# Order of the first loads and first products, and the queue of six stores, in an attention and MLP kernel

## The chip, the core and the metric

The kernel runs on one core of one Trainium2 chip. A core has TensorE (PE, matrix products into the PSUM memory), VectorE (DVE), ScalarE (ACT), GpSimd (POOL) and SyncE (SP). Each takes its instructions in program order and waits for others through semaphores. DMAs are issued from an engine's queue, here SP's and ScalarE's, and are carried out by 16 DMA engines. The metric is device microseconds of one execution; less is better.

## What is computed

One transformer block over 2048 rows of 512 numbers, in float32:

```python
x = A_x                                                  # 1 x 2048 x 512
h  = x + attention(layernorm(x), wqkv) @ wo              # 32 heads of 16, softmax over all 2048 keys
h2 = h + silu(layernorm(h) @ w1) @ w2                    # w1: 512 x 1792, w2: 1792 x 512
```

## The kernel before

Every float32 operand of a product is split into a high part and a low part (the rest), and a product is made as three: high by high, low by high, high by low. `low` (line 123) is the subtraction that makes a low part. The helpers `mm`, `tr`, `act`, `dve`, `pool`, `dma` (SP's queue) and `dma_beside` (ScalarE's queue), lines 97 to 121, pin each instruction to its place in program order on its engine, so the order of the calls in the text is the order of the work. The profile gives the helper's line: L98 is a matrix product, L101 a transposition on PE, L105 GpSimd, L112 ScalarE, L115 VectorE, L118 and L121 DMA issues from ScalarE and SP.

The rows are worked in four blocks of 512, each of four tiles of 128 rows.

**The start (lines 636 to 730).** The first block is made apart, with float32r operands, so that PE has work early. SP issues 20 loads of 256 KB: four tiles of x (`load_x`), four chunks of the values' weights (`raw_v`, 128 of the 512 input features each), eight chunks of the weights of keys and queries, and four tiles of the second block of x. The order of the first eight is x tile 0, x tile 1, value weight 0, x tile 2, value weight 1, x tile 3, value weights 2 and 3. In the trace x of this block lies in a buffer called `ks`, the raw weights in one called `va`. Then:

- `idle(20)` and `idle(4)` transpose the identity matrix on PE; their results are not used.
- `statistics` (line 211) takes mean and variance of a tile on VectorE (`bn_stats`, `bn_aggr`) and their reciprocal deviation on GpSimd (two small instructions into `rs`).
- `first_rows(t)` normalizes tile t on VectorE, turns it on PE (four transpositions) and casts it out of PSUM on ScalarE into `xth0` (`xt_h` in the trace).
- The four chunks of the values' weights are cast to float32r (`wv0_h`): chunks 0 and 3 on GpSimd, 1 and 2 on ScalarE. `low_v(c)` makes their low parts `wv0_l` on VectorE.
- `first_products(t, chunks)` adds the products of the high parts of tile t and of the chunks named into the PSUM bank of tile t. They are made by chunk: chunks 0 and 1 for tiles 0 and 1, chunk 2 for both, chunks 0 to 2 for tile 2, chunk 3 for tiles 0 to 2, all four for tile 3.
- The statistics of tiles 2 and 3 follow the normalization of the tile ahead of each. The low parts of weight chunks 0 and 1 stand between these steps, those of chunks 2 and 3 and of the four tiles of x at the end.

After that PE makes the products with the low parts (line 716 on), ScalarE evacuates the values and squares the raw weights, whose sums give the scales, and the second block's tiles are turned.

**The attention and MLP loop (line 1337 on).** PE makes scores, ScalarE exponentials, PE the products with the values; the maxima of the scores of later heads are found beside it by PE and VectorE (`maximum`, line 280; `mx` in the trace). When the heads of a block of rows are done, the block's MLP is run by `mlp(b)` (line 1114), for the first three blocks; the last has `finish_last`. `mlp` makes 14 chunks of first products, then second products in two passes over the 14 chunks: pass 0 for row tiles 0 and 1, pass 1 for tiles 2 and 3 (`pair_seconds`, line 1079, and `last_seconds`, line 1091). Bursts of maxima are put between them (`insert`, line 1145). The weights of the MLP lie split in DRAM (`w1d`, `w2d`) and are loaded over SP's queue, through a ring of eight buffers (`raw_tile`, tile `w`): a load waits until PE has left the buffer eight loads back. Pass 1 loads the second weights again.

`add_seconds` (line 1072) adds a finished tile to the rows on VectorE and issues the store of 256 KB to `out`; in pass 0 it is called at chunk 13 for each of two tiles, in `last_seconds` for the other two. All these stores go over SP's queue; only the second half of the very last tile (`m` = 1) goes over ScalarE's. `at["beside"]` is a flag that `mlp` sets at the head of each pair of chunks: true in all of pass 0 and in the first pairs of pass 1 (chunk below 4), false after that and everywhere else. `place_far` (line 333), which sends maxima through DRAM, already picks its queue by it.

Of the kernel before, what the change touches and what calls it, by code (L numbers as in the profile page):

```python
# [20 lines left out]
P = 128  # L21
# [5 lines left out]
DC = D // P  # L27
# [11 lines left out]
LN = 2.0 ** 10  # L39
# [51 lines left out]
def attention_mlp_kernel(ctx: ExitStack, tc: tile.TileContext, x, wqkv, wo, w1, w2, out):  # L91
    nc = tc.nc
    x = x.flatten_outer_dims()
    out = out.flatten_outer_dims()


    def mm(*a, **k):
        tc.keep_in_program_order(nc.tensor.matmul(*a, **k))  # L98

    def tr(*a):  # L100
        tc.keep_in_program_order(nc.tensor.transpose(*a))  # L101


    def pool(op, *a, **k):
        tc.keep_in_program_order(getattr(nc.gpsimd, op)(*a, **k))  # L105


    def pin(ins):
        tc.keep_in_program_order(ins)

    def act(fn, *a, **k):
        pin(getattr(nc.scalar, fn)(*a, **k))  # L112

    def dve(fn, *a, **k):
        pin(getattr(nc.vector, fn)(*a, **k))  # L115
# [4 lines left out]
    def dma(*a):  # L120
        pin(nc.sync.dma_start(*a))  # L121

    def low(dst, src, high, engine="dve"):

        if high.dtype == F32R:
            high = high.bitcast(F32)
        (pool if engine == "pool" else dve)("tensor_tensor", dst, src, high, ALU.subtract)
# [40 lines left out]
    def bank(kind="st", dtype=F32):  # L168
        ps = space[:, next_bank(kind), :]
        return ps if dtype == F32 else ps.bitcast(dtype)[:, :512]  # L170
# [40 lines left out]
    def statistics(rows, scale=1.0):  # L211

        st = small.tile([P, 6], F32, name="st", bufs=5)
        mv = small.tile([P, 2], F32, name="mv", bufs=5)
        rs = small.tile([P, 1], F32, name="rs", bufs=5)
        dve("bn_stats", st, rows)
        dve("bn_aggr", mv, st)
        pool("tensor_scalar", rs, mv[:, 1:2], EPS, scale ** -2, op0=ALU.add, op1=ALU.mult)
        pool("tensor_tensor", rs, rs, expo, ALU.pow)
        return mv, rs  # L220

    def normalize(dst, rows, mv, rs, engine="dve"):
        (pool if engine == "pool" else dve)("tensor_scalar", dst, rows, mv[:, 0:1], rs, op0=ALU.subtract, op1=ALU.mult)
# [142 lines left out]
    at = {"item": 0, "done": 0, "half": 0, "step": 0, "due": 0, "attention": False, "group": None, "ready": 0, "next": 0, "blocks": True, "beside": False}  # L366
# [102 lines left out]
    with ExitStack() as pa:  # L469
# [13 lines left out]
        wv0_h, wv0_l, xth0, xtl0 = (wvp.tile([P, DC, 512], F32R, name=name) for name in ("wv0_h", "wv0_l", "xt0_h", "xt0_l"))  # L483

        xts = [ks[2 + b % 2].rearrange("p a n -> p (a n)").bitcast(F32).rearrange("p (t d) -> p t d", d=D)
               for b in range(NB)]
# [3 lines left out]
        flat = va.rearrange("p c h d -> p (c h d)")  # L490
        raw_v, *raw_qk = (flat[:, -n * DC * D:][:, :DC * D].rearrange("p (c n) -> p c n", c=DC) for n in (3, 2, 1))

        def load_x(b, parts=1, tiles=range(4)):
            n = 4 // parts
            for t in tiles[::n]:
                r0 = b * 512 + t * P
                dma(xts[b][:, t:t + n, :], x[r0:r0 + n * P, :].rearrange("(t p) d -> p t d", p=P))

# [132 lines left out]
        def turn_x(b, t):  # L631

            turn(xts[b][:, t, :], xth[b][:, :, t * P:(t + 1) * P], xtl[b][:, :, t * P:(t + 1) * P],
                 "sm" if b == 1 else "st")

        load_x(0, 4, range(1))
        for dc in range(DC):
            load_x(0, 4, range(4)[dc + 1:dc + 2])
            dma(raw_v[:, dc, :], wqkv[dc * P:(dc + 1) * P, 2 * D:])
        for key in (1, 0):  # L640
            for dc in range(DC):
                dma(raw_qk[key][:, dc, :], wqkv[dc * P:(dc + 1) * P, key * D:(key + 1) * D])
        load_x(1, parts=4)


        def columns(t):
            return slice(t * P, (t + 1) * P)

        def idle(n):
            ps = bank()  # L650
            for c in range(n):
                tr(ps[:, columns(c % 4)], ident, ident)

        def turn_high(b, t):
            ps = bank("sm").rearrange("p (c n) -> p c n", n=P)
            high = xth[b] if b else xth0
            for c in range(4):
                tr(ps[:, c, :], xts[b][:, t, c * P:(c + 1) * P], ident)
            act("copy", high[:, :, columns(t)], ps)
            return ps  # L660

        idle(20)
        found = [statistics(xts[0][:, t, :], LN) for t in range(2)]
        turned, ps_vs = [], []

        def first_rows(t):
            normalize(xts[0][:, t, :], xts[0][:, t, :], *found[t])
            turned.append(turn_high(0, t))

        def first_products(t, *chunks):  # L670
            if t == len(ps_vs):
                ps_vs.append(bank("st" if t < 3 else "sm"))
            for c in chunks:
                mm(ps_vs[t], xth0[:, c, columns(t)], wv0_h[:, c, :], start=c == 0, stop=False)

        def low_v(c):
            low(wv0_l[:, c, :], raw_v[:, c, :], wv0_h[:, c, :])

        first_rows(0)
        pool("tensor_copy", wv0_h[:, 0, :], raw_v[:, 0, :])  # L680
        idle(4)
        first_rows(1)
        act("copy", wv0_h[:, 1, :], raw_v[:, 1, :])
        found.append(statistics(xts[0][:, 2, :], LN))
        low_v(0)
        for c in range(2):
            for t in range(2):
                first_products(t, c)
        act("copy", wv0_h[:, 2, :], raw_v[:, 2, :])
        first_rows(2)  # L690
        found.append(statistics(xts[0][:, 3, :], LN))
        low_v(1)
        pool("tensor_copy", wv0_h[:, 3, :], raw_v[:, 3, :])
        for t in range(2):
            first_products(t, 2)
        first_products(2, 0, 1, 2)
        first_rows(3)
        for t in range(3):
            first_products(t, 3)
        first_products(3, *range(DC))  # L700
        for c in range(2, 4):
            low_v(c)
        for t in range(4):
            low(xtl0[:, :, columns(t)], turned[t], xth0[:, :, columns(t)])

# [4 lines left out]
        found = {}  # L710
# [24 lines left out]
        for b in range(NB):  # L735
# [6 lines left out]
            found = {}  # L742
# [81 lines left out]
        for g in range(1, NG // 2):  # L824
            for m, (b, key) in enumerate([(b, 1) for b in range(NB)] + [(b, 0) for b in range(NB)]):
# [3 lines left out]
                n = 8 * g + m - 12  # L829
# [3 lines left out]
                beside = {BESIDE_A1[m]: 6} if g == 1 and m < len(BESIDE_A1) else BESIDE_A  # L833
                if n >= 18:
                    beside = BESIDE_T[n - 18]
# [206 lines left out]
    def rows_of(b, t):  # L1042
        return ot[b % 2][:, t].rearrange("p c n -> p (c n)")
# [28 lines left out]
    def add_seconds(b, t, ps, m=0, parts=1):  # L1072

        n, h = 4 * b + t, rows_of(b, t)
        cols = slice(m * D // parts, (m + 1) * D // parts)
        dve("scalar_tensor_tensor", h[:, cols], ps, out_f, h[:, cols], op0=ALU.mult, op1=ALU.add)
        (dma_beside if m else dma)(out[n * P:(n + 1) * P, cols], h[:, cols])

    def pair_seconds(b, acc, tiles, f, gates):

        w2 = [ws.pop(("w2", k)) for k in (f, f + 1)]
        for t in tiles:
            rows = slice(t * P, (t + 1) * P)
            for k, ((gh, gl), (w2h, w2l)) in enumerate(zip(gates[f:f + 2], w2)):
                for x, w in ((gh, w2h), (gl, w2h), (gh, w2l)):
                    mm(acc[t], x[:, rows], w, start=f + k == 0 and w is w2h and x is gh, stop=f + k == FC - 1 and w is w2l)
                    yield
            if f + 2 == FC:
                add_seconds(b, t, acc[t])
# [85 lines left out]
    found = {}  # L1175
# [138 lines left out]
    def maxima(g):  # L1314

        i, c = divmod(g, KC)
        goals = [(64 * (n + 1), KC * n) for n in range(i + 1, LAST)]
        goals += [(END - 32 * (1 - a), KC * LAST + HALF * a) for a in range(2) if KC * LAST + HALF * a > g]
        ready = min(ITEMS, i + RING - (0 if c == KC - 1 else 1)) * 64
        rate = max([(n - sum(x for x, m in zip(BESIDE, marks) if g <= m <= start) - at["done"])  # L1320
                    / max(1, start - AHEAD - g) for n, start in goals] or [0])
        if ready < END:
            rate = min(rate, (ready - at["done"]) / (KC - 1 - c or KC))
        at["due"] += max(0, rate)
        if g < LAG or g in marks or g - 1 in marks:

            return 0
        at["ready"] = ready
        most = 2 if at["step"] in late or c == JOINT and i and i - 1 not in FIRSTS else 3
        n = max(0, min(most, int(at["due"]), ready - at["done"]))  # L1330
        at["due"] -= n
        return n
# [4 lines left out]
    for g in range(groups):  # L1337
        tick()
        i, c = divmod(g, KC)
# [13 lines left out]
        if i in FIRSTS:  # L1353
            b, n = i // 8 - 1, c - OUTPUT
# [23 lines left out]
        n = maxima(g)  # L1378
# [4 lines left out]
        beside = range(n)  # L1383
        if n == 3 and more < 0:
            beside = range(1, 4)
        if n == 2 and more > 0:
            beside = 0, 2
# [52 lines left out]
```

## Time and profile before

| | |
|---|---|
| median of 3 runs | 1601.46 us (1600.91 to 1601.49) |
| the profiled execution | 1600.8 us |
| its span, first to last instruction | 1599.0 us |
| granted clock of TensorE | 1.00 |
| DMA, mean over the span | 86 GB/s |

In the rows of a timeline the first column is the start in microseconds from the span's start, the second the duration; then engine, line, operation and tiles, how many instructions are merged, and in brackets the idle time ahead of it and what ended it. A row of the waits reads: who waited for whom, us in total, times, longest. A row of a stretch gives its length and then the busy time of PE, PE's weight loads, VectorE, ScalarE and GpSimd, each with its number of instructions, the granted clock, the share of the DMA engines and GB/s.

### The profile page before, as it was taken

Reading aid. Unit: us, or ns where it says so; the run is one execution under the profiler, and the core shown is the slowest. Engines: PE = TensorE matmul, PEld = TensorE weight load, DVE = VectorE, ACT = ScalarE, POOL = GpSimd, SP = SyncE. Lnnn points to the kernel's source line nnn. Section 1 sums busy time; section 2 is a strip of 40 time slices with the busy share of each in tenths; the row PEclk is TensorE's granted clock in tenths of the full one; section 3 lists DMA queues with packets and bytes.
Section 4 is the critical chain, followed back from the end, with each engine's and each line's share of the span. In section 5 each row is a group of like instructions: output and inputs, shape, how many; then the busy total and the mean of one; then the engine's idle time right before and its main releaser. Section 6 shows DMA issues by size and latency. Waiting matters only on the chain.

```text
span 1599.0 us, 28492 instructions
## 1 busy us (share of the span) xinstructions
PE 1585.4 (99%) x10524; PEld 478.1 (30%) x10524; DVE 1389.5 (87%) x2053; ACT 1206.8 (75%) x2385; POOL 472.8 (30%) x755
## 2 busy tenths in 40 slices
PE   9999999999999999999999999999999999999999
PEld 6433322222234322222233322222234322222254
DVE  7999999999989889999989889999987789998432
ACT  5545799999964179999973179999974189999732
POOL 5643544544426101211135201211126101211200
PEclk9999999999999999999999999999999999999999
DMA  6667533442423521121123421112123511100222
GB/s 212 169 174 224 139 86 90 112 129 77 114 72 100 150 55 35 38 56 38 50 75 100 143 62 33 39 44 50 49 76 106 159 39 37 34 12 22 74 86 73
DMA packets 111427, 137.15 MB, mean 86 GB/s; under 512 B 29136, under 2 KB 66064, under 8 KB 111288
## 3 DMA queue, kind: packets, MB, share of 16 engines
q1 hardware_dynamic: 105844, 126.74, 28.8%
q10 hardware_dynamic: 5444, 8.59, 1.9%
q8 instruction: 82, 1.34, 0.4%
q14 instruction: 57, 0.47, 0.1%
HBM read 104.68 MB, written 24.85 MB: 81 GB/s over the span
## 4 chain that ended last, share of the span: by engine, by line
PE 83%; ACT 9%; DVE 5%; issue 1%; DMA 1%; POOL 1%; SPq 0%; POOLq 0%; ACTq 0%
PE ps L98 82%; ACT pt L112 9%; DVE mx L294 2%; DVE mx L296 1%; PE ps L101 1%; DVE pvs L115 0%; POOL rs L105 0%; DVE st L115 0%; DVE htl L115 0%; DVE hx L115 0%; DMA w<-w2d 0%; DMA md<-mt 0%; DVE ks L115 0%; POOL wv_l L105 0%; DMA ks<-in_A_x_dram 0%
## 5 line engine op out<-in xcount | busy, mean ns | idle before, releaser
L112 ACT ACTIVATE pt<-ps 128x512 f32<-128x512 f32 x2048 | 1009.0, 616 | 148.7 <-PE ps L98 146.7
L296 DVE TENSOR_REDUCE mx<-ps 128x1 f32<-128x512 f32 x1470 | 924.7, 683 | 51.6 <-PE ps L98 23.3
L98 PE MATMUL ps<-pt,va 128*17 128x512 f32 x4096 | 537.6, 598 | 0.9
L98 PE MATMUL ps<-qs,ks 64*128 64x512 f16 x2048 | 531.6, 380 | 2.4 <-DVE htl L115 0.7
L98 PE MATMUL ps<-ks,qs 48*128 48x512 f16 x2048 | 493.9, 381 | 1.5 <-DVE mx L294 1.1
L294 DVE TENSOR_REDUCE mx<-ps 128x2 f32<-128x1024 f32 x289 | 334.9, 1218 | 43.1 <-PE ps L98 41.8
L98 PEld LDWEIGHTS <-ks 64*128 64x128 f16 x2048 | 149.8, 95 | 545.5 <-issue 429.1
L105 POOL TENSOR_TENSOR ri<-rc,minus 128x16 f32<-128x16 f32 x31 | 90.7, 2925 | 235.3 <-DMA rc<-dn 168.7
L98 PE MATMUL ps<-w,gh 128*128 128x512 f16 (+1 forms) x678 | 154.6, 378 | 1.0 <-DMA w<-w2d 1.0
L98 PEld LDWEIGHTS <-qs 48*128 48x128 f16 x2048 | 126.6, 95 | 76.1 <-issue 59.7
L98 PEld LDWEIGHTS ps<-pt,va 128*17 128x17 f32 x4096 | 69.2, 95 | 223.6 <-issue 205.0
L98 PE MATMUL ps<-hth,w 128*128 128x512 f16 (+1 forms) x472 | 133.0, 370 | 0.0
L112 ACT ACTIVATE g<-ps,factors 128x512 f32<-128x512 f32 x56 | 38.4, 686 | 123.8 <-PE ps L98 96.7
L105 POOL TENSOR_TENSOR mx<-mx 128x32 f32<-128x32 f32 x52 | 12.4, 239 | 395.9 <-DVE mx L296 389.3
L98 PEld LDWEIGHTS <-w 128*128 128x128 f16 x708 | 66.2, 98 | 80.1 <-issue 12.5
L98 PEld LDWEIGHTS <-gh 128*128 128x128 f16 x678 | 63.0, 98 | 83.1 <-issue 13.7
L98 PE MATMUL ps<-htl,w 128*128 128x512 f16 (+1 forms) x236 | 84.1, 369 | 0.0
L115 DVE SCALAR_TENSOR_TENSOR gh<-g,factors,gh 128x512 f16<-128x512 f32 x14 | 10.5, 752 | 52.1 <-ACT gh L112 52.1
L112 ACT ACTIVATE ks<-ps 128x512 f32<-128x512 f32 x30 | 17.9, 598 | 49.2 <-PE ps L98 43.4
L105 POOL TENSOR_TENSOR sl<-ks,sh 128x512 f16<-128x512 f32 x30 | 34.6, 1156 | 51.6 <-ACT sh L112 32.5
L105 POOL TENSOR_TENSOR gh<-g,gh 128x512 f16<-128x512 f32 x42 | 48.5, 1155 | 3.5
L105 POOL TENSOR_TENSOR ot<-ot,den 128x512 f32<-128x512 f32 (+1 forms) x16 | 20.4, 1275 | 89.2 <-DMA den<-dr 72.8
(154 smaller groups left out, 974.3 us busy)
## 6 DMA issues: line engine op xcount, KB each, us to landing
w<-w2d SPq DMA_DIRECT2D x98, 256.0 KB
ks<-kd SPq DMA_DIRECT2D x120, 192.0 KB
w<-w1d SPq DMA_DIRECT2D x56, 256.0 KB
ks<-in_B_w_dram ACTq DMA_DIRECT2D x28, 256.0 KB
w<-in_B_w_dram SPq DMA_DIRECT2D x28, 256.0 KB
qs<-qd SPq DMA_DIRECT2D x128, 48.0 KB
kd<-sh SPq DMA_DIRECT2D x16, 256.0 KB
qd<-sh SPq DMA_DIRECT2D x16, 256.0 KB
```

Of the source, the lines that this page charges most:

```text
L98: tc.keep_in_program_order(nc.tensor.matmul(*a, **k))
L101: tc.keep_in_program_order(nc.tensor.transpose(*a))
L105: tc.keep_in_program_order(getattr(nc.gpsimd, op)(*a, **k))
L112: pin(getattr(nc.scalar, fn)(*a, **k))
L115: pin(getattr(nc.vector, fn)(*a, **k))
L294: pin(nc.vector.tensor_reduce(of, space[:, n:n + 2, :], axis=AX.X, op=ALU.max))
L296: pin(nc.vector.tensor_reduce(of[:, j:j + 1], space[:, n, :], axis=AX.X, op=ALU.max))
```

## The change

It has two parts. In the start, x's four tiles are all loaded ahead of the four chunks of the values' weights. The statistics of tile 2 now stand ahead of the normalization of tile 1, those of tile 3 ahead of the normalization of tile 2. Weight chunk 0 is cast on ScalarE, chunk 1 on VectorE, chunks 2 and 3 on GpSimd. The first products follow the tiles as they come, and all four low parts of the weights are made at the end on VectorE. In the MLP, `add_seconds` also uses ScalarE's queue while the flag is true: that holds for the two stores of pass 0, in each of three blocks.

```diff
-        def load_x(b, parts=1, tiles=range(4)):
+        def load_x(b, parts=1):
             n = 4 // parts
-            for t in tiles[::n]:
+            for t in range(0, 4, n):
...
-        load_x(0, 4, range(1))
+        load_x(0, parts=4)
         for dc in range(DC):
-            load_x(0, 4, range(4)[dc + 1:dc + 2])
             dma(raw_v[:, dc, :], wqkv[dc * P:(dc + 1) * P, 2 * D:])
...
-        def low_v(c):
-            low(wv0_l[:, c, :], raw_v[:, c, :], wv0_h[:, c, :])
-
         first_rows(0)
-        pool("tensor_copy", wv0_h[:, 0, :], raw_v[:, 0, :])
         idle(4)
+        found.append(statistics(xts[0][:, 2, :], LN))
+        act("copy", wv0_h[:, 0, :], raw_v[:, 0, :])
         first_rows(1)
-        act("copy", wv0_h[:, 1, :], raw_v[:, 1, :])
-        found.append(statistics(xts[0][:, 2, :], LN))
-        low_v(0)
-        for c in range(2):
-            for t in range(2):
-                first_products(t, c)
-        act("copy", wv0_h[:, 2, :], raw_v[:, 2, :])
+        found.append(statistics(xts[0][:, 3, :], LN))
+        first_products(0, 0)
         first_rows(2)
-        found.append(statistics(xts[0][:, 3, :], LN))
-        low_v(1)
-        pool("tensor_copy", wv0_h[:, 3, :], raw_v[:, 3, :])
+        dve("tensor_copy", wv0_h[:, 1, :], raw_v[:, 1, :])
+        for c in range(2, 4):
+            pool("tensor_copy", wv0_h[:, c, :], raw_v[:, c, :])
+        first_products(1, 0)
         for t in range(2):
-            first_products(t, 2)
-        first_products(2, 0, 1, 2)
+            first_products(t, 1)
+        first_products(2, 0, 1)
         first_rows(3)
         for t in range(3):
+            first_products(t, 2)
+        first_products(3, 0, 1, 2)
+        for t in range(4):
             first_products(t, 3)
-        first_products(3, *range(DC))
-        for c in range(2, 4):
-            low_v(c)
+        for c in range(DC):
+            low(wv0_l[:, c, :], raw_v[:, c, :], wv0_h[:, c, :])
         for t in range(4):
             low(xtl0[:, :, columns(t)], turned[t], xth0[:, :, columns(t)])
...
-        (dma_beside if m else dma)(out[n * P:(n + 1) * P, cols], h[:, cols])
+        (dma_beside if m or at["beside"] else dma)(out[n * P:(n + 1) * P, cols], h[:, cols])
```

## Prediction, made before the changed kernel was seen

> **What bounds the kernel now.** I read the head of the page first, then the waits of PE over the whole run, then PE's busy time in stretches.
>
> ```profile
> span 1599.0 us, 28492 instructions
> ...
> PE 1585.4 (99%) x10524; PEld 478.1 (30%) x10524; DVE 1389.5 (87%) x2053; ACT 1206.8 (75%) x2385; POOL 472.8 (30%) x755
> ```
> ```profile
> PE ps L98 <- DVE mx L294: 1.1, 4, 0.3
> PE ps L98 <- DMA w<-w2d: 1.0, 1, 1.0
> ```
> ```profile
> 5.00:10.00 5.00, 4.50 (x22) 3.06 (x22) 3.63 (x8) 2.21 (x4) 2.77 (x6) 1.00 1.03 379
> 10.00:15.00 5.00, 4.16 (x20) 2.64 (x20) 4.24 (x8) 2.10 (x3) 1.67 (x3) 1.00 1.05 391
> ```
>
> The reader is to see that TensorE has work nearly always: 1599.0 - 1585.4 = 13.6 us without it. So an edit can win only where PE waits, or where PE is kept from its next piece of work by an order of instructions. Two such places touch this change: the first 15 us (0.50 and 0.84 us without work in the two stretches shown, at a granted clock of 1.00), and one wait of 1.0 us for a second-product weight, the only one in the run. The profiled execution took 1600.8 us, 1.8 us around its span; the median shown, 1601.46, lies 0.66 above it. Differences are worked out on the trace and taken from the median.
>
> **Part 1: the start.** First the DMAs. SP issues all 20 loads of the start in one line; the change moves the third and fourth tiles of x from places 4 and 6 to places 3 and 4, and the four value weights from 3, 5, 7, 8 to 5, 6, 7, 8. Nothing else in SP's queue moves.
>
> ```profile
> 0.72 0.86 SPq L121 DMA_DIRECT2D ks<-in_A_x_dram  x2
> ...
> 3.52 6.26 SPq L121 DMA_DIRECT2D va<-in_A_wqkv_dram  x10
> ```
> ```profile
> GB/s 0 33 281 315 184 371 383 369 379 391 399 395 385 389 385 387 381 391 371 102 16 0 0 0 0 0 0 0 112 282 53 313 385 360 301 37 0 102 106 111
> ```
>
> The second fence has 1 us per number. Each transfer is 0.262 MB, so the running sum reaches transfers 3, 4, 5, 6, 7, 8 at about 4.9, 5.6, 6.3, 7.0, 7.7 and 8.4 us. The first is full by the sum at 2.8 us; VectorE first reads it at 3.44 us, 0.6 later, so I add 0.6 for landing (estimate): x's third tile at 5.5, its fourth at 6.2, the weights at 6.9, 7.6, 8.3, 9.0. The stream then runs on at the same rate to 19 us whatever the order of its first eight.
>
> Now the engines, each in order:
>
> ```profile
> 5.31 0.55 DVE L115 TENSOR_SCALAR ks<-ks,mv,rs 128x512 f32<-128x512 f32 x1 [0.17 <-POOL rs L105]
> 6.31 0.81 DVE L115 TENSOR_SCALAR ks<-ks,mv,rs 128x512 f32<-128x512 f32 x1 [0.45 <-POOL rs L105]
> 7.04 0.68 DVE L115 BATCH_NORM_STATS2 st<-ks 128x6 f32<-128x512 f32 x1
> 7.75 0.18 DVE L115 BATCH_NORM_AGGREGATE mv<-st 128x2 f32<-128x6 f32 x1
> ...
> 9.24 0.55 DVE L115 TENSOR_SCALAR ks<-ks,mv,rs 128x512 f32<-128x512 f32 x1 [0.72 <-POOL rs L105]
> ...
> 11.92 0.81 DVE L115 TENSOR_SCALAR ks<-ks,mv,rs 128x512 f32<-128x512 f32 x1 [0.72 <-POOL rs L105]
> 12.65 1.28 DVE L115 TENSOR_TENSOR wv_l<-va,wv_h 128x512 fp32r<-128x512 f32 x2
> 13.86 2.47 DVE L115 TENSOR_TENSOR xt_l<-ps,xt_h 128x512 fp32r<-128x512 f32 x4
> ```
> ```profile
> 5.63 0.64 POOL L105 TENSOR_TENSOR rs<-rs,expos 128x1 f32<-128x1 f32 x1
> 6.23 0.61 POOL L105 CAST wv_h<-va 128x512 fp32r<-128x512 f32 x1
> 8.03 0.55 POOL L105 TENSOR_SCALAR rs<-mv 128x1 f32<-128x1 f32 x1 [1.19 <-DVE mv L115]
> 8.66 0.55 POOL L105 TENSOR_TENSOR rs<-rs,expos 128x1 f32<-128x1 f32 x1
> ```
> ```profile
> 6.91 0.58 ACT L112 CAST xt_h<-ps 128x512 fp32r<-128x512 f32 x1 [4.91 <-PE ps L101]
> ...
> 8.35 1.14 ACT L112 CAST wv_h<-va 128x512 fp32r<-128x512 f32 x2
> ...
> 13.48 0.59 ACT L112 CAST xt_h<-ps 128x512 fp32r<-128x512 f32 x1 [2.35 <-PE ps L101]
> ...
> 21.18 1.07 ACT L112 ACTIVATE va<-ps 128x512 f32<-128x512 f32 x2
> ```
> ```profile
> 12.79 0.66 PE L101 MATMUL ps<-ident,ks 128*128 128x128 f32 x4 [0.64 <-DVE ks L115]
> 13.20 2.12 PE L98 MATMUL ps<-wv_h,xt_h 128*128 128x512 f32 x7
> 15.16 1.07 PE L98 MATMUL ps<-wv_l,xt_h 128*128 128x512 f32 x4
> 16.07 1.07 PE L98 MATMUL ps<-wv_h,xt_l 128*128 128x512 f32 x4
> ...
> 22.42 1.03 PE L101 MATMUL ps<-ident,ks 128*128 128x128 f32 x8
> ```
>
> The chain before: for each tile VectorE takes statistics, GpSimd makes the reciprocal deviation, VectorE normalizes, PE turns. The statistics of a tile stand right ahead of its own normalization, so GpSimd's two steps (8.03 to 9.21) lie open on VectorE, with a low part put between. The change puts the statistics of tile 3 ahead of the normalization of tile 2, and so on, and sends all four low parts behind. By the rows:
>
> - Tile 3's statistics follow the first normalization (5.86): 0.68 + 0.18, to 6.70. Its x, at 5.5, is there.
> - Second normalization 6.72 to 7.27: 0.55, as GpSimd casts nothing beside it now (0.81 when it did). Before it ended at 7.12: 0.15 lost.
> - Fourth tile's statistics to 8.1. GpSimd's steps for tile 3 (0.55 + 0.55) end at 8.0, so the third normalization runs 8.1 to 8.7 (before 9.24 to 9.79).
> - The new VectorE copy of a weight, 128x512: no row of its own. Below it can't be nothing; the nearest rows are 0.55 (the normalization, the same shape from SBUF) and 0.64 (1.28 for two subtractions). I take 0.55, to 9.25, with 0.3 to 0.8 as ends. The copy on ScalarE costs 1.14 / 2 = 0.57, at 7.5 behind the first turned tile, off the chain.
> - GpSimd's steps for tile 4 run 8.15 to 9.3; fourth normalization 9.35 to 10.15 (0.81, since the two GpSimd casts start beside it), before 11.92 to 12.73.
> - PE: turned tile 2 from 7.3, first product 8.1, turned tile 3 from 8.75, its cast done 1.28 after (13.48 + 0.59 - 12.79), at 10.0; two products; turned tile 4 from 10.5 (before 12.79).
> - Its cast is done at 11.8; seven products are left behind it, where four were. Four products take 16.07 - 15.16 = 0.91, so seven take 1.6. The first product with a low weight starts at 13.5, before 15.16: **1.65 us earlier**.
>
> What could be late next: the four low weights on VectorE, 10.15 + 4 x 0.64 = 12.7, before 13.5. The low rows follow (0.62 each) from 12.7, first needed at 13.5 + 0.91. ScalarE's run of casts and squares, which ended with the pair at 21.18 close ahead of PE's 22.42, starts 13.48 - 11.2 = 2.3 earlier. The second block's x keeps landing until 17, 0.6 behind the sum, and its second normalized tile is needed by PE at 20.8. From there all work hangs on PE's products, so the gain stays.
>
> A row to weigh a rule on: the normalization takes 0.81 instead of 0.55 where it runs beside GpSimd's cast (6.31 against 6.23 to 6.84). The Trainium skill, SBUF — State Buffer, Who interferes with whom, says that VectorE copies and tensor-scalars in their two-port mode and GpSimd block each other for a whole instruction. The trace agrees: 6.84 + 0.28 = 7.12, the end of that row. This speaks against moving a copy to VectorE and two casts beside it; at worst, by that rule, the fourth normalization loses to both casts, 9.3 + 1.22 + 0.28 = 10.8, and the gain is 1.3.
>
> So part 1 is worth -1.65, with ends 0 (the copy, the locks and the landings each at their worst) and -2.3 (all that the fourth turned tile gains).
>
> **Part 2: the stores.** Six stores of 256 KB, two in each of three blocks, go from SP's queue to ScalarE's.
>
> ```profile
> 1264.58 0.61 PE L98 MATMUL ps<-ks,qs 48*128 48x512 f16 x4
> ...
> 1273.06 0.38 PE L98 MATMUL ps<-w,gh 128*128 128x512 f16 x1 [1.00 <-DMA w<-w2d]
> ```
> ```profile
> 1264.77 1.73 ACTq L118 DMA_DIRECT2D md<-mt  x4
> ...
> 1265.39 3.26 SPq L121 DMA_DIRECT2D out_dram<-ot  x2
> ...
> 1267.54 0.74 DVE L115 SCALAR_TENSOR_TENSOR ot<-ps,factors,ot 128x512 f32<-128x512 f32 x1
> 1268.00 0.54 ACTq L118 DMA_DIRECT2D qs<-md  x2
> 1268.74 7.63 SPq L121 DMA_DIRECT2D w<-w2d  x9
> ...
> 1273.80 3.49 DVE L294 TENSOR_REDUCE mx<-ps 128x2 f32<-128x1024 f32 x3 [1.56 <-PE ps L98]
> ...
> 1284.35 2.06 ACT L112 ACTIVATE pt<-ps 128x512 f32<-128x512 f32 x4 [39.09 <-PE ps L98]
> ```
>
> This is the third block. SP sits on the second store until VectorE has added the rows (1267.54 + 0.74), and only then issues the load that PE waits for: 1268.74 to 1273.02, 4.3 us. That load is the weight of chunk 5 of the second pass, and takes the buffer of chunk 11 of the first, which PE leaves some 12 products ahead of the four at 1264.58, at about 1261.9. With the stores gone from SP it is issued there; even at 4.3 us it lands by 1266.2, 6 us early. The next two loads need chunks 12 and 13, free by 1264.6, and are wanted after 1273.8. **1.0 us** goes. Its successor would be VectorE, which waits 1.56 us for PE there and about 0.4 at the other bursts, so no new wait of PE is due. In the first two blocks PE never waits for this weight (the row with 1 wait in the run): nothing is won there.
>
> On ScalarE two DMA issues of some 0.4 us stand behind the two of the maxima (done 1268.54), so the stores go out up to 3 us later; nothing reads them. Behind them is the exponential of 1284.35, after 39.09 us of waiting for PE: that cover of 15 us hides the wait for VectorE's addition; if it were gone, each block would pay up to the 3 us for which SP sat there. Part 2 is -1.0, with ends 0 and -1.0.
>
> **Sum:** -1.65 - 1.0 = -2.65; 1600.8 - 2.65 = 1598.15 by the profiled execution, 1601.46 - 2.65 = 1598.8 by the median.
>
> **Rivals.**
> - *The stores' move saves nothing.* The bytes still share the engines, and a wait of the same size follows. Against it: the stream there is no wall, SP is held by VectorE and not by bytes. The time: 1601.46 - 1.65 = 1599.8. The Trainium skill, DMA: Bandwidth & Descriptors, Issuing engines are not separate DMA queues, says that another issuing engine saves only issue time; what SP loses here is a wait in front of the issue, which that rule doesn't count. Chance 0.1.
> - *The start gives nothing:* the port locks and the longer tail of seven products eat the shorter chain. For it: three more products stand behind the last cast. Against it: 2.3 us of chain against 0.7 of products. The time: 1601.46 - 1.0 = 1600.5. Chance 0.1.
> - *The start gives all:* turned tile 4 and the tail both at their best, -2.3 - 1.0 or a little more, 1598.1. Chance 0.12.
> - *Slower: the value weights land late.* VectorE's copy of the second weight stands ahead of the fourth normalization and of every low part, so a weight that lands after 8.7 holds all of VectorE. To lose the 2.65 and 3.2 us more, the last weight must land some 6 us behind its need at about 12.6: 18.5. That is 2.1 MB in 16 us, 130 GB/s. The lowest microsecond of the stream has 184, among 315 and 371; a lasting fall is not to be seen. The time: 1601.46 + 3.4 = 1604.9. Chance 0.04.
>
> **How the numbers follow.** The forecast, both parts near the sums above, has 0.64, the rivals 0.1, 0.1, 0.12 and 0.04. Predicted 1598.8. The range goes from 1597.8 (both best ends, -3.3, and 0.35 for the spread of the runs) to 1600.8 (only one part, and the spread); it leaves out the slower rival and the tails. About 0.2%, 3.2 us, is what a measurement of this kernel can tell from no change: 1598.26 and below is faster. The fourth case and the lower quarter of the forecast, some 0.1 + 0.1, lie there: 0.2. Slower 0.04; the rest, 0.76, is within it.
>
> **What would show it.** In the profile after: the low-weight products start near 13.5 and the eight turns of 22.42 near 20.8; VectorE's normalizations at about 6.7, 8.1 and 9.4; PE's wait for the second-product weight is gone, and the load ahead of it stands near 1260 on SP; six stores on ScalarE's queue, its exponentials no later against PE. Wrong would be: a VectorE row before 9 us whose idle time is ended by a value weight's DMA, a PE wait for VectorE's maxima in place of the one removed, or a start gained by 21 us that is no longer there at 100.

## The result, and the profile after

The changed kernel takes 1598.55 us (median of 18 runs, 1598.02 to 1599.25) where the kernel before takes 1601.53 us beside it (18 runs, 1600.76 to 1602.51): a ratio of 0.9982, with a 95% interval of 0.9974 to 0.9989. That is 3.0 us less; 1598.8 was forecast, and the time lies within 0.2% of before. The profiled execution took 1598.55 us, with a span of 1596.7 us, 2.3 less than the span of before.

The head of the page after and the waits of PE over the whole run (who waited for whom, us in total, times, longest):

```profile
span 1596.7 us, 28487 instructions
...
PE 1585.3 (99%) x10524; PEld 477.6 (30%) x10524; DVE 1389.7 (87%) x2054; ACT 1207.2 (76%) x2384; POOL 472.6 (30%) x755
```
```profile
PE ps L101 <- POOL ident masks.py:199: 1.5, 1, 1.5
PE ps L98 <- DVE mx L294: 1.0, 4, 0.3
PE ps L101 <- DVE hx L115: 0.8, 4, 0.3
PE ps L98 <- ACT wv_h L112: 0.7, 1, 0.7
PE ps L98 <- DVE htl L115: 0.7, 3, 0.2
```

PE does the same work in the same busy time; 11.4 us of its span are empty now, 13.6 before. The wait for a second-product weight is gone from the list, and a new one of 0.7 us for the cast of a value weight stands in it.

The start, first as busy time by stretch, then the rows of VectorE, ScalarE and PE that answer to those of before:

```profile
5.00:10.00 5.00, 4.25 (x25) 3.38 (x24) 4.19 (x11) 2.00 (x4) 3.76 (x8) 1.00 0.99 361
10.00:15.00 5.00, 5.00 (x23) 3.61 (x22) 5.00 (x9) 3.75 (x6) 1.25 (x3) 1.00 1.05 388
```
```profile
5.51 0.55 DVE L115 TENSOR_SCALAR ks<-ks,mv,rs 128x512 f32<-128x512 f32 x1 [0.17 <-POOL rs L105]
5.97 0.69 DVE L115 BATCH_NORM_STATS2 st<-ks 128x6 f32<-128x512 f32 x1
...
6.79 0.52 DVE L115 TENSOR_SCALAR ks<-ks,mv,rs 128x512 f32<-128x512 f32 x1
...
8.23 0.51 DVE L115 TENSOR_SCALAR ks<-ks,mv,rs 128x512 f32<-128x512 f32 x1
8.72 0.43 DVE L115 CAST wv_h<-va 128x512 fp32r<-128x512 f32 x1
9.59 0.81 DVE L115 TENSOR_SCALAR ks<-ks,mv,rs 128x512 f32<-128x512 f32 x1 [0.45 <-POOL rs L105]
10.33 2.90 DVE L115 TENSOR_TENSOR wv_l<-va,wv_h 128x512 fp32r<-128x512 f32 x4
```
```profile
8.05 0.62 ACT L112 CAST wv_h<-va 128x512 fp32r<-128x512 f32 x1 [0.30 <-DMA va<-in_A_wqkv_dram]
```
```profile
8.72 0.50 PE L98 MATMUL ps<-wv_h,xt_h 128*128 128x512 f32 x1 [0.70 <-ACT wv_h L112]
...
10.91 0.60 PE L101 MATMUL ps<-ident,ks 128*128 128x128 f32 x4
11.26 2.81 PE L98 MATMUL ps<-wv_h,xt_h 128*128 128x512 f32 x10
13.91 1.07 PE L98 MATMUL ps<-wv_l,xt_h 128*128 128x512 f32 x4
...
21.17 1.03 PE L101 MATMUL ps<-ident,ks 128*128 128x128 f32 x8
```

The idle time ended by GpSimd ahead of VectorE's third normalization (0.72 before) is gone; the fourth starts at 9.59 where it started at 11.92. From 10 to 15 us PE has no empty time left by the profile's count (it was busy for 4.16 of the 5 us before). The products with the low weights start at 13.91 instead of 15.16, and the eight turns at 21.17 instead of 22.42: 1.25 us in this execution. The gain stays: the reload of ScalarE's table at the first MLP, first in before, then in after,

```profile
475.69 1.28 ACT L112 ACT_TABLE_LOAD   x1
```
```profile
474.45 1.28 ACT L112 ACT_TABLE_LOAD   x1
```

is 1.24 us earlier still. The third block's second products after, all engines:

```profile
1256.87 17.21 SPq L121 DMA_DIRECT2D w<-w2d  x12
...
1267.02 0.54 ACTq L118 DMA_DIRECT2D qs<-md  x2
...
1267.62 3.49 DVE L294 TENSOR_REDUCE mx<-ps 128x2 f32<-128x1024 f32 x3 [0.46 <-PE ps L98]
1267.65 0.85 ACTq L118 DMA_DIRECT2D out_dram<-ot  x2
...
1271.51 3.49 DVE L294 TENSOR_REDUCE mx<-ps 128x2 f32<-128x1024 f32 x3 [0.40 <-PE ps L98]
...
1282.07 2.07 ACT L112 ACTIVATE pt<-ps 128x512 f32<-128x512 f32 x4 [37.91 <-PE ps L98]
```

SP issues twelve weight loads on end, with no store between; the stores go out from ScalarE behind the two transfers of the maxima, and its next exponential still waits 37.91 us for PE. From one burst of maxima to the next VectorE counts 1271.51 - 1267.62 = 3.89 us, where before it was 1273.80 - 1268.75 = 5.05: 1.16 us less. That is the idle microsecond and 0.16 beside it.

### The profile page after: what moved, and what is told of

It reads as the page before. It is cut to its first block, busy times and chain, and to the rows that moved or that the text cites. A ratio compares the mean times of both kernels' runs of the same rounds, so it can differ in the third digit from the quotient of the medians.

```text
span 1596.7 us, 28487 instructions
## 1 busy us (share of the span) xinstructions
PE 1585.3 (99%) x10524; PEld 477.6 (30%) x10524; DVE 1389.7 (87%) x2054; ACT 1207.2 (76%) x2384; POOL 472.6 (30%) x755
## 4 chain that ended last, share of the span: by engine, by line
PE 71%; ACT 22%; DVE 4%; DMA 1%; issue 1%; POOL 1%; SPq 0%; POOLq 0%; ACTq 0%
PE ps L98 70%; ACT pt L112 22%; DVE mx L294 2%; DVE mx L296 1%; PE ps L101 1%; DMA va<-in_A_wqkv_dram 0%; DMA ks<-in_A_x_dram 0%; DVE st L115 0%; DVE htl L115 0%; DVE hx L115 0%; SPq L121 0%; POOL rs L105 0%; POOL wv_l L105 0%; DVE xtl L115 0%; DVE ot L115 0%
## 5 line engine op out<-in xcount | busy, mean ns | idle before, releaser
L98 PEld LDWEIGHTS <-gh 128*128 128x128 f16 x678 | 63.1, 98 | 83.0 <-issue 13.7
```

## Experiments

Each kernel was timed against before on the same chip, 11 runs each. The intervals are about 0.0009 wide to each side, 1.4 us, so a difference of one microsecond is read from the traces, and the times are only asked not to contradict them. "First low product" is the start of the first product with a low weight; "wait" is PE's wait for the second-product weight of the third block.

| kernel | median, before beside it (us) | ratio, interval | span | first low product | wait |
|---|---|---|---|---|---|
| start_only | 1599.12, 1601.13 | 0.9988, 0.9978 to 0.9997 | 1597.8 | 13.84 | 0.7 |
| stores_only | 1599.73, 1601.13 | 0.9992, 0.9983 to 1.0001 | 1598.5 | 15.09 | none |
| order_only | 1600.18, 1601.13 | 0.9994, 0.9985 to 1.0003 | 1599.2 | 14.03 | 1.6 |
| loads_only | 1601.46, 1601.13 | 1.0004, 0.9995 to 1.0013 | 1599.0 | 15.28 | 0.9 |
| statistics_only | 1600.37, 1601.10 | 0.9996, 0.9987 to 1.0005 | 1599.0 | 14.72 | 1.5 |
| statistics_and_turn | 1600.21, 1601.78 | 0.9993, 0.9984 to 1.0002 | 1598.7 | 14.02 | 1.2 |
| wait_no_bytes | 1600.04, 1600.74 | 0.9995, 0.9986 to 1.0004 | 1598.2 | 15.53 | 0.2 |
| twice_the_bytes | 1599.71, 1600.74 | 0.9993, 0.9984 to 1.0002 | 1598.2 | 15.19 | none |
| stores_later | 1599.71, 1600.74 | 0.9994, 0.9985 to 1.0003 | 1598.1 | 15.17 | none |
| after_again | 1598.32, 1601.10 | 0.9984, 0.9975 to 0.9993 | 1596.8 | 13.48 | none |
| last_loads_later | 1597.76, 1601.10 | 0.9980, 0.9971 to 0.9989 | 1595.7 | 13.24 | none |

### The two parts apart

**start_only** is the change without its last line:

```diff
-        (dma_beside if m or at["beside"] else dma)(out[n * P:(n + 1) * P, cols], h[:, cols])
+        (dma_beside if m else dma)(out[n * P:(n + 1) * P, cols], h[:, cols])
```

> The whole first part of the change (order of the loads, of the statistics, of the casts and of the products), with the six stores back on SP. Theory: the two parts are independent. The start keeps its 1.25 us (first product with a low weight near 13.9, eight turns near 21.2 instead of 22.42), and PE's wait of about 1.0 us for a second-product weight in the third block is back. Time about 1600.2, span 1597.8. Rival, that the start's gain is given back later: eight turns near 21.2 but a span near 1599.0.

**stores_only** is before with that line alone changed.

> Only the six stores go to ScalarE's queue; the start is that of before. Theory: SP was held by the wait for VectorE's addition in front of the store, so the load behind it is issued near 1262 instead of 1268.7, and the third block gains 1.15 us (the idle microsecond and the pipeline's refill); the first two blocks gain nothing. Time about 1600.4, span 1597.8. Rival, that the stores' bytes on the same 16 DMA engines are the delay: PE's wait for the weight stays near 1.0, span 1599.0.

The two are independent but for 0.3 us. Alone, the start moves the first low product to 13.84 and leaves the wait; the stores alone remove the wait and leave the start. The medians fall by 2.0 and 1.4 us, together 3.4, beside 3.0 and 2.8 for both in one; within the intervals these agree. The span of stores_only, 1598.5, is 0.7 above what was expected: another wait, near 1488 us, met below, took 1.0 us of PE's time in its profiled execution and none in that of before.

The exception is this: from the table reload near 887 us to that near 1195 us the profile after takes 308.6 us and that of before 308.2. It is not one odd execution: after_again and last_loads_later, two more profiles with both parts, met below, take 308.5, and the ten profiles of kernels that lack one of the parts take 308.2 to 308.3. The loss lies at one place. Below are ScalarE's rows there, two of after and then one of start_only:

```profile
1143.05 0.65 ACTq L118 DMA_DIRECT2D qs<-mn  x1
1144.04 27.59 ACT L112 ACTIVATE pt<-ps 128x512 f32<-128x512 f32 x56 [0.36 <-PE ps L98]
```
```profile
1143.50 27.55 ACT L112 ACTIVATE pt<-ps 128x512 f32<-128x512 f32 x56
```

Behind the issue of a small transfer ScalarE's exponentials stand still for 0.36 us in after and for 0.40 in the other two; in the ten others there is no such gap. ScalarE's program in these three is the only one with both one cast fewer, from the new start, and six issues of stores more. Whether that makes the gap is not known.

### What in the start does it

**order_only** keeps the new order of statistics, casts and products, with the loads of before:

```diff
-        load_x(0, parts=4)
+        load_x(0, 4, range(1))
         for dc in range(DC):
+            load_x(0, 4, range(4)[dc + 1:dc + 2])
             dma(raw_v[:, dc, :], wqkv[dc * P:(dc + 1) * P, 2 * D:])
```

> The new order of statistics, casts and products, with the loads interleaved as before and the stores on SP. Theory: landings come about 0.7 us apart, the fifth at 8.05 in the trace after, so the third tile of x as fourth transfer lands near 7.35 and holds VectorE in front of the second normalization (5.97 to 7.35), the fourth tile as sixth near 8.75; the first product with a low weight starts near 14.5: about half of the start's gain is left, 0.6 of 1.25; time about 1600.8. Rival, that the order of the loads does not matter: 13.9 and 1600.2, as with the whole first part.

**loads_only** is the opposite: before, with x loaded ahead of the weights.

> Only the order of the loads: x first, then the values' weights; statistics, casts, products and stores as before. Theory: the first weight chunk lands near 8.05, GpSimd's cast of it moves from 6.23 to 8.05 and holds the deviation of the third tile behind it, so the third normalization moves from 9.24 to about 9.9 and the first product with a low weight from 15.16 to about 15.8: slower by 0.7, time about 1602.2. Rival, that x ahead of the weights is a gain by itself: below 15.16 and below 1601.5.

Both expectations missed. loads_only loses 0.1 (15.28), not 0.7. order_only has its first low product at 14.03, where 14.5 was expected; that is 0.1 to 0.8 behind the four profiles with the whole new start (13.91, 13.84, 13.48, 13.24) and 0.4 behind their mean. What failed is the rule of thumb of 0.7 us for each place in the queue, counted back from the one landing at 8.05. VectorE's row of order_only and GpSimd's of loads_only show landings:

```profile
6.40 0.69 DVE L115 BATCH_NORM_STATS2 st<-ks 128x6 f32<-128x512 f32 x1 [0.61 <-DMA ks<-in_A_x_dram]
```
```profile
7.32 0.61 POOL L105 CAST wv_h<-va 128x512 fp32r<-128x512 f32 x1 [0.85 <-DMA va<-in_A_wqkv_dram]
8.01 0.69 POOL L105 TENSOR_SCALAR rs<-mv 128x1 f32<-128x1 f32 x1
```

The third tile of x, now the fourth transfer, landed at 6.40 (7.35 expected), and VectorE waited 0.61 us for it. With x loaded first that wait is 0.32 us in start_only and nothing in the other three profiles. So, together with the new order of the work, the loads are worth some 0.4 us; alone, in loads_only, they gain nothing. The medians allow more: that of order_only lies 1.1 us above that of start_only, which differs from it in the loads alone, but this is within their intervals. The first weight as fifth transfer landed at 7.32, and GpSimd's next step started at 8.01 as it had at 8.03 before: it had waited for VectorE there, so the late cast cost nothing.

**statistics_only** takes before and moves two calls:

```diff
         idle(4)
+        found.append(statistics(xts[0][:, 2, :], LN))
         first_rows(1)
+        found.append(statistics(xts[0][:, 3, :], LN))
...
-        found.append(statistics(xts[0][:, 2, :], LN))
...
-        found.append(statistics(xts[0][:, 3, :], LN))
```

> From before, one edit: the statistics of tiles 2 and 3 each stand one normalization earlier on VectorE; loads, casts, products and stores are those of before. Theory: this hides GpSimd's steps behind VectorE's work and is the whole gain of the start; the fourth normalization moves from 11.92 to about 9.9, its turned tile to about 11.3, and the first product with a low weight starts at 13.6 to 13.8, as in the whole first part (13.84 and 13.91) or a little ahead; time about 1.3 below before. Rival, that the products tile by tile and the casts on other engines are needed for it: 14.5 or later.

A miss: 14.72, not 13.7. VectorE came near what was expected: it waited 0.56 us for the third tile of x, and the fourth normalization starts at 10.35, where about 9.9 was expected and 11.92 was before. PE did not follow it:

```profile
6.51 0.69 DVE L115 BATCH_NORM_STATS2 st<-ks 128x6 f32<-128x512 f32 x1 [0.56 <-DMA ks<-in_A_x_dram]
...
10.35 0.83 DVE L115 TENSOR_SCALAR ks<-ks,mv,rs 128x512 f32<-128x512 f32 x1
```
```profile
11.60 0.97 PE L98 MATMUL ps<-wv_h,xt_h 128*128 128x512 f32 x3 [0.21 <-ACT xt_h L112]
12.41 0.60 PE L101 MATMUL ps<-ident,ks 128*128 128x128 f32 x4
12.76 2.12 PE L98 MATMUL ps<-wv_h,xt_h 128*128 128x512 f32 x7
14.72 1.08 PE L98 MATMUL ps<-wv_l,xt_h 128*128 128x512 f32 x4
```

The fourth tile is normalized at 10.35 + 0.83 = 11.18, and its turning starts at 12.41, behind three products of the third tile that wait for ScalarE. **statistics_and_turn** changes only that:

```diff
-        first_products(2, 0, 1, 2)
         first_rows(3)
+        first_products(2, 0, 1, 2)
```

> The kernel with only the statistics moved, and one edit more: the turning of tile 4 is put ahead of tile 3's three products on PE instead of behind them; casts, loads and stores are those of before. Theory: in that kernel the fourth normalization was done at 11.18 and its turning started only at 12.41, since PE, in order, had tile 3's products ahead, which wait for ScalarE's cast of tile 3, itself held by two weight casts; with the turning ahead it starts near 11.3, and the first product with a low weight near 14.1 instead of 14.72. Rival, that the rest of the gain is due to the place of the weight casts: about 14.7 again.

```profile
11.24 0.66 PE L101 MATMUL ps<-ident,ks 128*128 128x128 f32 x4
11.66 2.53 PE L98 MATMUL ps<-wv_h,xt_h 128*128 128x512 f32 x10
14.02 1.07 PE L98 MATMUL ps<-wv_l,xt_h 128*128 128x512 f32 x4
```

The turning starts at 11.24, right behind the normalization, and the first low product at 14.02, as expected. So two small moves carry 1.1 of the gain: 0.4 for the statistics, 0.7 for turning the last tile ahead of products that are held up anyway. order_only, which has the same loads and, beyond these moves, the new places of the casts, stands at 14.03: by these two profiles the casts add nothing. The rest, from 14.0 to the mean of 13.6 with the whole new start, goes with the order of the loads.

### What the stores held up

**wait_no_bytes** is stores_only, and for each of the six stores a tiny one on SP that waits for the same addition:

```diff
+        if at["beside"]:
+            dma(spare[n * P:(n + 1) * P, :1], h[:, :1])
```

> The start of before, the six stores on ScalarE's queue, and for each of them a store of 512 bytes on SP's queue to a spare tensor, which waits for the same addition on VectorE. It adds those six small stores. Theory, SP held by the wait: the load behind is late again and PE's wait of about 1.0 us in the third block is back, span about 1599.0. Rival, bytes on the DMA engines: with nearly no bytes on SP no wait comes back, span 1597.8.

**twice_the_bytes** is stores_only with each store done a second time:

```diff
+        if at["beside"]:
+            dma_beside(spare[n * P:(n + 1) * P, :], h)
```

> The start of before, the six stores on ScalarE's queue, and each done a second time into a spare tensor over the same queue: 1.5 MB more in all. Theory, SP held by the wait: no change against the stores alone, no wait of PE for the weight, span about 1597.8. Rival, bytes: a wait of PE for weights returns, span 1598.5 or more.

**stores_later** leaves the stores on SP, behind six more loads:

```diff
+        if at["beside"]:
+            stores.append(store)
...
+                if part and f == 4:
+                    while stores:
+                        stores.pop(0)()
```

> The start of before; the six stores stay on SP's queue but are issued behind six more loads of the second pass instead of ahead of them. Theory: what matters is what stands behind the wait, not which engine issues; the wait of PE in the third block is gone as with ScalarE's queue, span about 1597.8. Rival, that ScalarE's queue itself is what helps: the wait of about 1.0 stays, span 1599.0.

Twice the bytes on ScalarE's queue bring back no wait, and stores on SP behind the loads do as well as on ScalarE: what matters is what stands behind the store. (The spans of these two, 1598.2 and 1598.1, lie 0.4 and 0.3 above what was expected; the wait near 1488 us took 0.7 and 0.4 us in them.) But wait_no_bytes brought back only 0.2 us of PE's wait and not 1.0. Its rows on SP and VectorE:

```profile
1265.48 3.24 SPq L121 DMA_DIRECT2D spare<-ot  x2
1268.83 7.08 SPq L121 DMA_DIRECT2D w<-w2d  x9
```
```profile
1268.84 3.49 DVE L295 TENSOR_REDUCE mx<-ps 128x2 f32<-128x1024 f32 x3 [0.46 <-PE ps L98]
1273.07 3.49 DVE L295 TENSOR_REDUCE mx<-ps 128x2 f32<-128x1024 f32 x3 [0.74 <-PE ps L98]
```

SP sits on the tiny stores just as long, and issues the load at 1268.83, as late as before (1268.74). Yet the burst follows after 4.23 us, where 5.05 were needed with the full stores and 3.89 without any. Of the 1.16 us some 0.3 come from the late issue by itself. The other 0.8 are put down to the bytes of the second store, which lie ahead of the load on the same queue. The first store is through by then: in before the DMA engines move 209 and 322 GB/s in the two half microseconds from 1266.0 to 1267.0, which is one store of 0.26 MB, and no more than 8 GB/s from there to 1269.0. In wait_no_bytes both full stores go out from ScalarE's queue from 1268.30 on, around the load, and move beside it; what differs is the queue. This rests on one profile, but its wait of 0.2 lies below all six with full stores on SP ahead of the load (0.7 to 1.6). Against those six, whose bursts follow after 4.73 to 5.67 us, the share of the bytes is 0.5 to 1.4 us. The late issue is the condition for both: in twice_the_bytes, where the load is issued early, the bytes cost nothing.

### A third wait of the same kind

**after_again** is the changed kernel once more.

> The changed kernel itself once more. Theory: the same start (first product with a low weight at 13.8 to 14.0) and no wait of PE for the weight of the third block; the wait for the last maxima near 1488, which took between 0 and 1.24 us in the eight profiles so far, falls anywhere in this span, and with it the span between 1596.5 and 1597.8.

The first low product came at 13.48, earlier than expected; the rest came as expected. The median is 2.8 us below that of before. PE's wait for the last maxima was 0.9 us in it; over all profiles here it is between 0 and 1.2.

```profile
PE ps L98 <- DMA qs<-mn: 0.9, 1, 0.9
```

The rows of the first profile after, all engines, show how these maxima are sent:

```profile
1482.10 1.38 SPq L121 DMA_DIRECT2D w<-w1d  x3
...
1483.27 0.65 ACTq L118 DMA_DIRECT2D qs<-mn  x1
...
1483.53 0.43 SPq L121 DMA_DIRECT2D w<-w2d  x1
...
1484.06 0.69 SPq L121 DMA_DIRECT2D qs<-mn  x1
```

The last maxima go out as two small transfers, one from ScalarE's queue, one from SP's; SP has four weight loads of 256 KB ahead of its own. That transfer was issued 0.79 us behind ScalarE's here and 1.85 in order_only, which has the longest wait. But the delay alone does not set the wait: it was 0.70 in twice_the_bytes, where PE waited 0.7 us, and 1.58 in wait_no_bytes, where PE did not wait. Why the wait wanders is not shown. **last_loads_later** moves those loads:

```diff
-            if c == 4:
+            if c == 6:
                 for f in range(3):
                     load_weights("w1", f)
```

> The changed kernel, and the four weight loads of the last MLP issued from SP two groups later, so that they no longer stand ahead of the store of the last maxima in SP's queue. Theory, the same as for the six stores (SP's order, not the number of bytes): the small transfer is issued right behind ScalarE's twin, lands about 2 us later, and PE's wait for it near 1488 is gone, also the 1 us that its weight loads wait; time 0.3 to 1.0 below the changed kernel, about 1598.0 where that one has 1598.5. Rival, that the transfer is late by its own latency: the wait stays within 0 to 1.2 and the time is the changed kernel's.

```profile
1482.30 0.69 SPq L121 DMA_DIRECT2D qs<-mn  x1
1482.30 0.65 ACTq L118 DMA_DIRECT2D qs<-mn  x1
...
1483.03 1.61 SPq L121 DMA_DIRECT2D w<-w1d  x3
...
1484.68 0.43 SPq L121 DMA_DIRECT2D w<-w2d  x1
```

Both transfers go out at once, and neither PE nor its weight loads wait for them any more. Whether the place in SP's order or the loads' bytes made the wait, this does not tell apart. The median is 1597.76 us (1597.50 to 1598.04), 0.6 below after_again beside it (1598.32, 1597.78 to 1598.97), and the runs lie within 0.5 us where the others spread over 1.2. It is the fastest kernel of this study.

## Why the prediction was right, point by point

- *The sum.* 2.65 us forecast; 3.0 and 2.8 measured by the medians, 2.3 by the two profiled spans. The medians show more than the spans because the profiled execution of before, 1600.8, lay near the low end of that kernel's runs. The third wait cost PE nothing in it, which may be the reason, but this is not shown: in the profile after it cost nothing either, and that execution lies at the median of its runs. That the sum came within 0.35 us is in part luck: the 0.3 us that the two parts cost together were in no term, and part 2 gave more than its term.
- *Part 1, 1.65.* The first low product came at 13.91, 13.84, 13.48 and 13.24 with the new start, mean 13.6 (13.5 forecast), and at 15.16, 15.09, 15.53, 15.19 and 15.17 with the old, mean 15.2: 1.6 us. The chain on PE was worked out rightly: from the turning of the third tile to that of the fourth it took 1.85 to 1.90 us (1.75 forecast), from there to the first low product 2.98 to 3.00 (3.0 forecast; the last sum, 11.8 + 1.6, gives 13.4 where 13.5 was written). The steps on VectorE came as worked out: normalizations at 6.79, 8.23 and 9.59 (6.72, 8.1, 9.35), and the fourth takes 0.81 beside GpSimd's casts.
- *The copy on VectorE,* taken at 0.55, took 0.43.
- *A step that was off:* the landing of the first weight, put at 6.9 by the sum of the bytes and 0.6. It landed at 8.05 in the profile after, and PE waited 0.70 us for its cast; in after_again ScalarE's cast of it started at 7.33, without a wait. The sum of bytes gives an order of landings, and no time to half a microsecond. It cost some 0.25 us in that execution: the third tile was normalized at 8.23 + 0.51 = 8.74 and turned only from 9.06, behind the late product, where in the other three profiles with the new start the turning follows the normalization within 0.06 us. In those, VectorE's chain up to the third tile sets PE's time.
- *Part 2, 1.0.* The stage became 1.16 us shorter, a little more than the end of 1.0 that was given. With the stores on SP ahead of the loads, PE's wait was 1.0, 0.7, 1.6, 0.9, 1.5 and 1.2 us in six profiles, mean 1.15: the one wait that the forecast had to go by lay near the mean, and could have been 0.7 or 1.6. ScalarE hid the wait for the addition as forecast.
- *A reason that was half wrong:* that SP "is held by VectorE and not by bytes". The wait for VectorE made the issue late, but by wait_no_bytes the late issue alone costs 0.3 of the 1.16 us, and the bytes of the second store ahead of the load the other 0.8.
- *The rivals.* None came: both parts gained, the weights' landing held VectorE nowhere, and no wait of PE for VectorE took the place of the one removed (1.0 us over the run, 1.1 before).
- *Missed:* the 0.3 us near 1144 us that the two parts lose together. The prediction took the parts as a plain sum; the cause is open.

## What to carry to other kernels

A store that waits for a late result belongs on a queue on which nothing urgent stands behind it, or behind the urgent loads on its own queue; both were equally good here. Look in a queue's timeline for the issue that sits longest, and ask what stands behind it and who waits for that: the same reading found a third place, which the change had not touched. On an engine that works in order, take the short step that feeds a round trip through other engines ahead of bulk work: the statistics and the turning of the last tile were worth 1.1 us, the order of the loads some 0.4, and that only behind them.

## What the runs showed of the hardware

The landing of 256 KB transfers queued back to back varied from execution to execution about as much as by a place in the queue. The first tile of x was read between 3.33 and 3.64 us over all profiles (3.44 before and 3.64 after, with its issue at 0.72 in both); the first value weight, as fifth transfer, was there at 8.05 (after), 7.32 (loads_only) and no later than 7.33 (after_again). The third tile of x, as third transfer, was there by 5.97, 5.93 and 5.70 in three profiles and landed at 6.29 in start_only; as fourth it landed at 6.40, 6.51 and 6.52 (order_only, statistics_only, statistics_and_turn).

With a 256 KB store just ahead of it on its own queue, a load was there 0.8 us later than with a store of 512 bytes there, one profile against one.

VectorE's normalization of a 128x512 tile and GpSimd's cast of one hinder each other, and the second to start pays. In before the normalization starts second (6.31 against 6.23) and takes 0.81 us, the cast 0.61; in wait_no_bytes and twice_the_bytes it starts first (6.54 against 6.75, 6.30 against 6.43) and takes 0.55, the cast 0.81 and 0.89.
